# One product of a first-layer pair split into seven smaller ones, with the work around it moved

## The chip, the cores and the metric

The kernel runs on one core of a Trainium2 chip. The core has a matrix engine (TensorE, PE in the profile, with its weight loads shown as PEld), a vector engine (VectorE, DVE), a scalar engine (ScalarE, ACT), a general engine (GpSimd, POOL) and a queue that issues transfers (SyncE, SP). Each takes its instructions in order and waits on semaphores for the others. TensorE writes its results to PSUM, which the kernel uses as eight banks of 512 fp32 words in each of 128 partitions; everything else is in SBUF. The metric is the device time of one execution in microseconds (us), as a median over runs.

## The reference, cut to what matters

```
kv  = einsum('bhsd,bhse->bhde', k, v)    # per batch b (8) and head h (8): k^T v, 64 x 64, over s = 576
out = q kv ; out = out / sqrt(mean(out^2) + 1e-6) * g_norm
x   = out as (B*S, H*D)                  # 4608 tokens x 512 features
y   = (sigmoid(x @ w_gate) * (x @ w_val)) @ w_out     # 512 -> 1536 -> 512, all fp32
```

The two matrix layers of the last line are most of the work. w_gate and w_val are 512 x 1536, w_out is 1536 x 512.

## The kernel before, in words

**Chunks.** The 4608 tokens are cut into nine chunks of 512 (`G`). Chunk 0 is computed plainly while the attention of the first two batches and the conversion of the weights run beside it. Chunks 1 to 8 go through `first_layer_fast(c)` (line 684) and `second_layer_fast(c)` (line 768), in which a product of 2 x 2 blocks is made of seven block products instead of eight, with sums of blocks of x, of the weights and of the results in place of the eighth.

**First layer.** The features are 12 blocks of 128; a pair is block `one` = f and block `two` = f + 6, and there are six pairs in a chunk, so 48 pairs in the eight fast chunks. For each block the 2 x 2 cut of x is by token half (256 tokens, `GH`) and by half of the 512 inputs; that of the weights is by half of the inputs and by gate or value. The seven products are called `p1, p6, p2, p7, p5, p4, p3` and are issued in this order, each for `one` and then for `two`. Each is two matmuls of 128 x 128 weights against 128 x 256 of x (`product`, line 692, the matmul itself on line 694), accumulated in one PSUM bank. An fp32 matmul shows in the profile as two passes, each with a weight load of its own, so a product is four passes and a pair has 56.

`p1` goes to a new bank `pa` and ScalarE copies it (line 702). `p2` adds to `pa`, and ScalarE takes the sigmoid of it for the first token half (line 712). `p6` goes to a new bank `pb`, `p7` and `p4` add to it, and `p5` opens the bank `pc`, to which `p3` adds. After `p6`, `p7`, `p5`, `p4` and `p3` VectorE adds the bank to a sum in SBUF (lines 708, 716, 721, 725, 730), after `p4` ScalarE takes the second sigmoid (line 726). `end` (line 733) multiplies values by gates, 512 wide, once for each block and after all products of the pair, and `h_sums` (lines 763 to 766) forms four sums of results for the second layer, each 256 wide and with both operands in SBUF. Banks are taken in turn from two pools of two (`mm_ps`), four banks in all: the next pair's `p1` goes to the banks of `pb`, its `p6` to those of `pc`. The other four banks are one tile `at` for the attention.

**Weight sums.** `w_sum` (line 677, the instruction on line 681) runs on GpSimd: four subtractions of 128 x 256 for each block, eight in a pair, for the pair that follows. Those of a kind have two buffers, one for each block of a pair, so a sum for the next pair is written when the product that reads the old one is done. They are issued after `p5` (three for each block) and after `p4`.

**Slots.** `feed(b)` makes a list of steps for the attention of batch b = c + 1, and `spread` lays them into a queue `fill`; `slot()` takes one step from it. There are seven slots in a pair (after each of the seven products of both blocks) and 28 in the second layer of a chunk, and a step is issued to its engine at that point of the program. Steps of VectorE go only into slots 2 to 5 of a pair (counted from 0), or 1 to 5 in chunk 1; other slots are left empty or hold a step of another engine. The steps are: turn q (`turn`, line 369, two for each of four head pairs), k^T v (`kv_mm`), its copies out of PSUM (`kv_copies`, line 364, on VectorE), then twice `two_pairs`: `u_mm` on TensorE, `u_square` on ScalarE (line 399), `u_sum` (line 402, two reductions), `u_root` (ScalarE), `u_norm` (line 411, two), and `x_turn` (line 418, two), which also issues the transfers on SP (line 428) that bring the result into the next chunk's x. What does not fit into the 42 slots of the first layer goes on in the second. `sums_of(c + 1)` puts the four x sums of the next chunk (lines 671 to 674) at the end of the queue. Chunks 1 to 6 carry a feed, chunks 7 and 8 none.

Of the kernel before, what the change touches and what calls it, by code (L numbers as in the profile page):

```python
# [20 lines left out]
def kernel(  # L21
# [319 lines left out]
    def feed(b):  # L341
# [4 lines left out]
        def kv_mm():  # L346
            mains, rest = kv_late[b]
            d["kv"] = ps = at_ps()
            for n in range(NHP):
                for j in range(NK4):  # L350
                    for e in range(2):
                        c = slice(NK4 * HD * e + HD * j, NK4 * HD * e + HD * j + HD)
                        nc.tensor.matmul(ps[HD * e:HD * e + HD, n, 0:HD], mains[n, "k"][:, c], mains[n, "v"][:, c],  # L353
                                         start=(j == 0), stop=False)
            for i in range(NHP // 2):
                for r in range(2):
                    for e in range(2):
                        n, rs, c = NHP // 2 * r + i, slice(PH * r, PH * r + PH), HD * (2 * i + e)
                        nc.tensor.matmul(ps[HD * e:HD * e + HD, n, 0:HD], rest[rs, c:c + HD],
                                         rest[rs, GH + c:GH + c + HD], start=False, stop=True)  # L360

        def kv_copies(i, rs):
            for r in rs:
                nc.vector.tensor_copy(out=kvq[QB * r:QB * r + QB, :, i], in_=d["kv"][QB * i:QB * i + QB, :, 0:HD])
# [80 lines left out]
        for i in range(2 * NC):  # L445
            for rs in ((0, 1), (2,)):
                steps.append((DVE, lambda i=i, rs=rs: kv_copies(i, rs)))
# [3 lines left out]
        return steps + [(PE, idle)] + turns_of(n0 + 3) + two_pairs(n0 + 2) + [(PE, idle)] * 5  # L451
# [50 lines left out]
    psum_mm = ctx.enter_context(tc.tile_pool(name="psum_mm", bufs=2, space=bass.MemoryType.PSUM))  # L502
    psum_ctx = tc.tile_pool(name="psum0", bufs=1, space=bass.MemoryType.PSUM)
    psum0 = psum_ctx.__enter__()

    def mm0_ps():
        return psum_mm.tile([P, 512], FP32, tag="mm", name="mm")

    turns = count()

    def mm_ps():
        if next(turns) % 4 < 2:
            return psum.tile([P, 512], FP32, tag="mm", name="mm", bufs=2)
        return mm0_ps()

    def at_ps():
        return psum.tile([P, 4, 512], FP32, tag="at", name="at")
# [145 lines left out]

    def quarters(c):
        return {(i, j): xT[c][:, NK * (j - 1):NK * j, GH * (i - 1):GH * i] for i in (1, 2) for j in (1, 2)}

    def x_sums(c):
# [6 lines left out]
            lambda: tt(out=s[:, 2], in0=a[1, 2], in1=s[:, 1], op=ALU.subtract),  # L674
        ]

# [7 lines left out]
    def first_layer_fast(c):  # L684
        s, a = sx[c], quarters(c)

        def block(f):

            d = {}
            bg, bv = w["wg", f], w["wv", f]  # L690

            def product(ps, wt, xs, new):
                for m in range(NK):
                    nc.tensor.matmul(ps, wt[:, m, :], xs[:, m, :], start=(new and m == 0), stop=(m == NK - 1),  # L694
                                     skip_group_check=True)


            def p1():
                d["pa"] = pa = mm_ps()[:, h1]
                product(pa, bg[:, 0:NK], a[1, 1], True)  # L700
                d["sg"] = sg_tile()
                nc.scalar.copy(out=d["sg"][:, h2], in_=pa)  # L702

            def p6():
                d["pb"] = pb = mm_ps()[:, h1]
                product(pb, tw[f, 2], s[:, 1], True)
                d["h"] = gv_tile(c, f)
                tt(out=d["h"][:, h1], in0=pb, in1=d["sg"][:, h2], op=ALU.add)

            def p2():  # L710
                product(d["pa"], bg[:, NK:], a[1, 2], False)
                nc.scalar.activation(out=d["sg"][:, h1], in_=d["pa"], func=AF.Sigmoid)  # L712

            def p7():
                product(d["pb"], tw[f, 3], a[2, 1], False)
                tt(out=d["h"][:, h2], in0=d["pb"], in1=d["sg"][:, h2], op=ALU.add)  # L716

            def p5():
                d["pc"] = pc = mm_ps()[:, h1]
                product(pc, tw[f, 1], s[:, 0], True)  # L720
                tt(out=d["h"][:, h2], in0=pc, in1=d["h"][:, h2], op=ALU.add)

            def p4():
                product(d["pb"], tw[f, 4], a[2, 2], False)
                tt(out=d["sg"][:, h2], in0=d["pb"], in1=d["sg"][:, h2], op=ALU.add)  # L725
                nc.scalar.activation(out=d["sg"][:, h2], in_=d["sg"][:, h2], func=AF.Sigmoid)  # L726

            def p3():
                product(d["pc"], bv[:, NK:], s[:, 2], False)
                tt(out=d["h"][:, h1], in0=d["pc"], in1=d["h"][:, h1], op=ALU.add)  # L730

            def end():
                tt(out=d["h"], in0=d["h"], in1=d["sg"], op=ALU.mult)  # L733

            return [p1, p6, p2, p7, p5, p4, p3], end

        for f in range(NF2):
            one, two = block(f), block(f + NF2)
            for i, (p, r) in enumerate(zip(one[0], two[0])):
                p()  # L740
                r()
                slot()

                if f + 1 < NF2 or c + 1 < NG:
                    n = (f + 1) % NF2
                    if i == 4:
                        for k_ in (1, 2, 3):
                            w_sum(n, k_)
# [147 lines left out]
```

## Time and profile before

| | |
|---|---|
| median of 9 runs (lowest, highest) | 1081.18 us (1080.71, 1082.5) |
| the profiled execution: its time, its span | 1081.27 us, 1079.4 us |
| TensorE busy, granted clock | 1068.4 us (99%), 0.997 |
| VectorE, GpSimd, ScalarE busy | 636.4, 291.1, 242.4 us |
| first-layer matmuls (line 694) on the chain that ended last | 53% of the span |
| second-layer matmuls (line 780) on it | 25% |

The profile is of one execution. A row of a timeline gives the start, the length from the first start to the last end, and how many instructions are merged in it; the distance from one start to the next is what an instruction costs a full queue, and the duration of a single one is longer, because the end of one overlaps the beginning of the next. A row of groups gives the mean duration of one instruction. The 1.87 us between the span and the time of the profiled execution lie before the first and after the last instruction.

### The profile page before, as it was taken

The page shows a single profiled execution, that of the slowest core. Times are in us where ns is not written, and L with a number is a line of the kernel's source. Part 1 is how long each engine was busy: PE and PEld are TensorE (multiplying, and loading weights), DVE is VectorE, ACT ScalarE, POOL GpSimd, SP SyncE. Part 2 cuts the span into 40 slices and gives each one's busy share as a digit, 9 for nine tenths or more (in the row PEclk, how much of TensorE's full clock was granted, in tenths as well). Part 3 has the DMA queues.
Part 4 walks back from the last instruction along what each step waited for, and adds up shares of the span by engine and source line. Part 5 has one row for each costly group of instructions (what it writes and reads, how often), then busy time and mean ns, then how long its engine had stood idle before and what let it go on. Part 6 is the DMA issues. An engine that isn't in the chain of part 4 may idle for free.

```text
span 1079.4 us, 18246 instructions
## 1 busy us (share of the span) xinstructions
PE 1068.4 (99%) x7226; PEld 886.0 (82%) x7226; DVE 636.4 (59%) x1261; ACT 242.4 (22%) x473; POOL 291.1 (27%) x390
## 2 busy tenths in 40 slices
PE   9999999999999999999999999999999999999997
PEld 8544448888888888888888888888888888888886
DVE  4897757783577437662767357844765266416631
ACT  4654321221113111221122112311131122002200
POOL 0000024440254124420444035402442054205500
PEclk9999999999999999999999999999999999999998
DMA  9944710002400240013201140024001200010001
GB/s 265 246 156 156 243 34 17 12 12 75 119 6 18 58 128 10 24 39 76 81 12 46 42 119 12 20 58 128 1 24 37 48 1 1 2 38 1 1 1 39
DMA packets 69108, 64.89 MB, mean 60 GB/s; under 512 B 23712, under 2 KB 63008, under 8 KB 69024
## 3 DMA queue, kind: packets, MB, share of 16 engines
q1 hardware_dynamic: 68768, 63.69, 20.9%
q8 instruction: 58, 0.95, 0.4%
q14 instruction: 26, 0.21, 0.1%
q10 hardware_dynamic: 256, 0.03, 0.1%
HBM read 47.19 MB, written 9.44 MB: 52 GB/s over the span
## 4 chain that ended last, share of the span: by engine, by line
PE 95%; DVE 2%; DMA 1%; issue 0%; SPq 0%; ACT 0%; DVEq 0%
PE mm L694 53%; PE mm L780 25%; PE mm L541 7%; PE mm L638 4%; PE at L393 2%; PE at L353 1%; PE at L541 1%; DVE gv L733 1%; PE two L291 1%; PE two L261 0%; PE mm L619 0%; PE two L318 0%; DVE qTs L369 0%; DMA q<-in_q_dram 0%; PE two L272 0%
## 5 line engine op out<-in xcount | busy, mean ns | idle before, releaser
L681 POOL TENSOR_TENSOR tw<-gv 128x256 f32<-128x256 f32 x192 | 139.4, 737 | 733.2 <-PE mm L694 581.8
L694 PE MATMUL mm<-xT,tw 128*128 128x256 f32 x768 | 182.1, 380 | 0.0
L694 PE MATMUL mm<-xT,gv 128*128 128x256 f32 x768 | 182.0, 380 | 0.0
L694 PE MATMUL mm<-sx,tw 128*128 128x256 f32 x768 | 181.6, 380 | 0.0
L694 PEld LDWEIGHTS mm<-xT,gv 128*128 128x128 f32 x768 | 145.8, 190 | 20.1 <-issue 0.5
L694 PEld LDWEIGHTS mm<-sx,tw 128*128 128x128 f32 x768 | 146.1, 190 | 19.6
L694 PEld LDWEIGHTS mm<-xT,tw 128*128 128x128 f32 x768 | 145.7, 190 | 19.7
L681 POOL TENSOR_TENSOR tw<-gv,tw 128x256 f32<-128x256 f32 x192 | 157.0, 839 | 0.0
L726 ACT ACTIVATE sg<-sg 128x256 f32<-128x256 f32 x96 | 39.7, 417 | 243.9 <-DVE sg L725 243.7
L733 DVE TENSOR_TENSOR gv<-gv,sg 128x512 f32<-128x512 f32 x96 | 93.7, 1014 | 0.0
L694 PE MATMUL mm<-sx,gv 128*128 128x256 f32 x384 | 90.7, 379 | 0.0
L780 PE MATMUL mm<-w,s 128*128 128x256 f32 (+1 forms) x408 | 88.6, 367 | 0.0
L780 PE MATMUL mm<-t2w,gv 128*128 128x256 f32 x384 | 88.1, 379 | 0.0
L780 PE MATMUL mm<-w,gv 128*128 128x256 f32 x384 | 88.1, 379 | 0.0
L716 DVE TENSOR_TENSOR gv<-mm,sg 128x256 f32<-128x256 f32 x96 | 40.8, 425 | 76.5 <-PE mm L694 76.3
L780 PEld LDWEIGHTS mm<-w,s 128*128 128x128 f32 x408 | 74.1, 191 | 9.3
L694 PEld LDWEIGHTS mm<-sx,gv 128*128 128x128 f32 x384 | 73.1, 190 | 9.8
L780 PEld LDWEIGHTS mm<-w,gv 128*128 128x128 f32 x384 | 73.1, 190 | 9.8
L780 PEld LDWEIGHTS mm<-t2w,gv 128*128 128x128 f32 x384 | 73.0, 190 | 9.7
L541 PE MATMUL mm<-xT,gv 128*128 128x512 f32 x176 | 77.4, 594 | 0.0
L702 ACT COPY sg<-mm 128x256 f32<-128x256 f32 x96 | 35.7, 372 | 156.5 <-PE mm L694 155.3
L712 ACT ACTIVATE sg<-mm 128x256 f32<-128x256 f32 x96 | 36.8, 383 | 125.5 <-PE mm L694 125.5
(96 smaller groups left out, 998.7 us busy)
## 6 DMA issues: line engine op xcount, KB each, us to landing
q<-in_q_dram SPq DMA_DIRECT2D x24, 288.0 KB
st<-in_moe_w_gate_dram SPq DMA_DIRECT2D x12, 512.0 KB
st<-in_moe_w_val_dram SPq DMA_DIRECT2D x12, 512.0 KB
st<-in_moe_w_out_dram SPq DMA_DIRECT2D x12, 512.0 KB
kv<-in_k_dram SPq DMA_DIRECT2D x24, 256.0 KB
kv<-in_v_dram SPq DMA_DIRECT2D x24, 256.0 KB
out_dram<-sg SPq DMA_DIRECT2D x23, 192.0 KB
xT<-xTs SPq DMA_DIRECT2D x48, 72.0 KB
```

The source lines that it names most:

```text
L291: nc.tensor.matmul(d["u"][r:r + PH, e, HD * (i // 2):HD * (i // 2) + HD], d["qT"][es, t0:t0 + PH], kv[es], start=True, stop=True)
L393: nc.tensor.matmul(u[HD * e:HD * e + HD, r, o:o + HD], qTs[QB * r:QB * r + QB, (n0 + which) % 2, c:c + PH], kvq[QB * r:QB * r + QB, (n0 + ...
L541: nc.tensor.matmul(self.ps[i], w[("wg", "wv")[i], self.f][:, m, :], xT[self.c][:, m, :], start=(m == 0), stop=(m == NMT - 1), skip_group_c ...
L638: nc.tensor.matmul(ps[t], gv[0, f][:, P * t:P * t + P], w["wo", f], start=(f == 0), stop=(f == NFT - 1), skip_group_check=True)
L681: nc.gpsimd.tensor_tensor(out=tw[f, i], in0=b[in0], in1=b[in1] if isinstance(in1, tuple) else tw[f, in1], op=ALU.subtract)
L694: nc.tensor.matmul(ps, wt[:, m, :], xs[:, m, :], start=(new and m == 0), stop=(m == NK - 1), skip_group_check=True)
L702: nc.scalar.copy(out=d["sg"][:, h2], in_=pa)
L712: nc.scalar.activation(out=d["sg"][:, h1], in_=d["pa"], func=AF.Sigmoid)
L716: tt(out=d["h"][:, h2], in0=d["pb"], in1=d["sg"][:, h2], op=ALU.add)
L726: nc.scalar.activation(out=d["sg"][:, h2], in_=d["sg"][:, h2], func=AF.Sigmoid)
L733: tt(out=d["h"], in0=d["h"], in1=d["sg"], op=ALU.mult)
L780: nc.tensor.matmul(ps, hs(f), ws[:, f, :], start=(new and f == 0), stop=(f == NF2 - 1), skip_group_check=True)
```

## The change

**The split.** `p2` of `one` and `p2` of `two` multiply the same quarter of x (second half of the inputs, first 256 tokens) with the gate weights of two blocks, so together they are a 256 x 256 by 256 x 256 product. It is now cut once more into 2 x 2 blocks of 128 and made of seven matmuls (`small`, each 128 x 128 weights against 128 x 128 of x) in place of four with 256 columns. Two of the seven add straight into the bank `pa` of `one`; the others go into a fifth bank `pd` (later `pe`). ScalarE copies partial results from it (four copies 128 wide), GpSimd adds two of them (one 256 wide), and VectorE makes three more additions (one 256 wide, two 128 wide). The sigmoid of the first token half now reads SBUF. The weights for it need four more subtractions a pair on GpSimd (`w_sums2`, 128 x 128), the x quarter four more sums a chunk on VectorE (`x_sums2`).

**Banks.** `at` shrinks from four banks to three, and five banks are handed out from a queue, `take` and `give`. `pc` of one block is now the bank of the other's `pa`. `pd` is the third bank in the queue when it is taken: at that point it is the one in which `p3` of `two` of the pair before has just ended.

**Order.** `p5` of `one` comes before `p7`, the weight sums are issued after `p5` of `two`, and `end` is split by token half: that of the second half stands ahead of `p3` of `one` for `one`, and ahead of `p3` of `two` for `two`, there together with the first of the four result sums (`h_sum`); that of the first half stays after all products, with the other three result sums.

**Feed.** The copies of k^T v go from VectorE to ScalarE and are no longer held to slots 2 to 5; the second `two_pairs` gets four empty steps ahead of it, and one of the five empty steps at the end is taken away.

```diff
-                nc.vector.tensor_copy(out=kvq[...], in_=d["kv"][QB * i:QB * i + QB, :, 0:HD])
+                nc.scalar.copy(out=kvq[...].rearrange("p (s n) d -> p s n d", s=2), in_=d["kv"][QB * i:QB * i + QB])
...
-        return steps + [(PE, idle)] + turns_of(n0 + 3) + two_pairs(n0 + 2) + [(PE, idle)] * 5
+        steps += [(PE, idle)] + turns_of(n0 + 3) + [(PE, idle)] * (4 if b > 2 else 0)
+        return steps + two_pairs(n0 + 2) + [(PE, idle)] * 4
...
-        return psum.tile([P, 4, 512], FP32, tag="at", name="at")
+        return psum.tile([P, NQ, 512], FP32, tag="at", name="at")
+    free = deque([4, 2, 3, 0, 1])
+    def take():
+        i = free.popleft()
+        return i, bank(i)[:, 0:GH]
+    def give(i):
+        free.append(i)
...
+        for i, in0, in1 in ((1, b12, b11), (2, b22, 1), (4, b21, 2), (3, b22, b12)):
+            tw2[i] = sums.tile([P, P], FP32, tag=f"tx{i}", name=f"tx{i}", bufs=1)
+            nc.gpsimd.tensor_tensor(out=tw2[i], in0=in0, in1=..., op=ALU.subtract)
...
+            p1(one)
+            p1(two)
+            slot()
+            i_d = free[2]
+            del free[2]
+            pd = bank(i_d)
+            small(pd[:, q1], ones[:, NK], ax[:, 0, q1], True)
+            nc.scalar.copy(out=g1[:, q1], in_=pd[:, q1])
+            small(one["pa"][:, q1], ones[:, NK + 1], ax[:, 1, q1], False)
+            p6(one)
+            small(pd[:, q1], tw2[2], s2[:, 1], False)
+            nc.scalar.copy(out=g2[:, q1], in_=pd[:, q1])
+            small(one["pa"][:, q2], tw2[4], ax[:, 1, q2], False)
+            p6(two)
+            slot()
+            small(pd[:, q1], tw2[3], ax[:, 0, q2], False)
+            nc.scalar.copy(out=g1[:, q2], in_=pd[:, q1])
+            nc.scalar.copy(out=g2[:, q2], in_=pd[:, q1])
+            nc.gpsimd.tensor_tensor(out=g2[:, h1], in0=g2[:, h1], in1=g2[:, h2], op=ALU.add)
+            tt(out=g1[:, h1], in0=one["pa"], in1=g1[:, h1], op=ALU.add)
+            nc.scalar.activation(out=g1[:, h1], in_=g1[:, h1], func=AF.Sigmoid)
+            p5(one, two["ia"])
+            slot()
+            p7(one)
+            pe = bank(i_d)
+            small(pe[:, q1], tw2[1], s2[:, 0], True)
+            tt(out=g2[:, q2], in0=pe[:, q1], in1=g2[:, q2], op=ALU.add)
+            slot()
+            p7(two)
+            p5(two, one["ia"])
+            slot()
...
+            p4(one)
+            small(pe[:, q1], twos[:, NK + 1], s2[:, 2], False)
+            tt(out=g2[:, q1], in0=pe[:, q1], in1=g2[:, q1], op=ALU.add)
+            nc.scalar.activation(out=g2[:, h1], in_=g2[:, h1], func=AF.Sigmoid)
+            p4(two)
+            give(i_d)
+            slot()
...
+            end(one, h2)
+            p3(one)
+            end(two, h2)
+            h_sum(c, f)
+            p3(two)
+            slot()
+            end(one, h1)
+            end(two, h1)
+            h_sums(c, f)
```

## The prediction

> **What bounds the kernel now.** Read first the busy times and the chain that ended last (two lines of the page), then whom TensorE waited for, then its timeline in a stretch of first-layer work and at the very end, where the only passes of 128 columns in the fast part stand.
>
> ```profile
> PE 1068.4 (99%) x7226; PEld 886.0 (82%) x7226; DVE 636.4 (59%) x1261; ACT 242.4 (22%) x473; POOL 291.1 (27%) x390
> ...
> PE 95%; DVE 2%; DMA 1%; issue 0%; SPq 0%; ACT 0%; DVEq 0%
> ```
>
> TensorE is the bound, and 95% of the chain is its own work.
>
> ```profile
> PE mm L619 <- POOL ident masks.py:199: 1.4, 1, 1.4
> PE two L291 <- ACT qTs L277: 0.6, 2, 0.3
> PE two L272 <- DMA q<-in_q_dram: 0.5, 1, 0.5
> ```
>
> These are all the waits of TensorE's matmuls, and none is of the fast layers (lines 694 and 780). So there is no wait to remove: only fewer columns can gain, and every new wait is a loss.
>
> ```profile
> 440.03 2.00 PE L694 MATMUL mm<-xT,tw 128*128 128x256 f32 x8
> 441.86 1.89 PE L694 MATMUL mm<-sx,gv 128*128 128x256 f32 x8
> 443.58 1.89 PE L694 MATMUL mm<-xT,gv 128*128 128x256 f32 x8
> 445.31 1.89 PE L694 MATMUL mm<-sx,tw 128*128 128x256 f32 x8
> ```
>
> ```profile
> 1063.41 2.84 PE L780 MATMUL mm<-w,s 128*128 128x128 f32 x24
> 1066.09 2.76 PE L780 MATMUL mm<-t2w,gv 128*128 128x256 f32 x12
> ```
>
> Sixteen passes of 256 columns go from 441.86 to 445.31: 0.216 us each. Twenty-four of 128 columns, each with its own 128 x 128 weight load, go from 1063.41 to 1066.09: 0.112 us each.
>
> **Step 1, the saving.** In a pair, p2 of both blocks is 4 matmuls = 8 passes x 0.2156 = 1.725 us. The seven small ones are 14 passes x 0.1117 = 1.563 us. Saved: 0.162 us a pair, x 48 pairs = **7.8 us**, all on the path.
>
> [...] This trace has 0.112 against 0.429 for 512 columns (line 541), 58.37 us for 136 passes on its chain, a ratio of 0.26: the weight loads are hidden here. [...]
>
> **Step 2, what VectorE, GpSimd and ScalarE get, and their shared cost.** VectorE, in a pair: one more addition of 256 (0.34 us from start to start in the rows below) and two of 128, which no row shows (bounds 0 and 0.34; nearest, by the slope from 512 wide, 0.60 in 444.13 to 444.73, to 256, 0.34: 0.21 each), and `end` in four parts of 0.34 for two of 0.60: +0.9 us. It loses 12 copies a chunk (72 x 420 ns in the group of line 364), which ScalarE, 22% busy, takes. GpSimd: eight subtractions x 0.69 = 5.5 us before; four of 128 (between 0.35, half of 0.69, and 0.69; I take 0.36, as its two sources scale with width) and one of 256 more: 7.6 us of the pair's 11.9 us (56 x 0.2156 - 0.162). None of this counts by itself: it lies beside TensorE. But look at how the two engines meet:
>
> ```profile
> 221.76 0.74 DVE L402 TENSOR_REDUCE ms<-sqs 128x9 f32<-128x576 f32 x1
> 222.42 0.41 DVE L725 TENSOR_TENSOR sg<-mm,sg 128x256 f32<-128x256 f32 x1
> ...
> 225.22 1.91 DVE L733 TENSOR_TENSOR gv<-gv,sg 128x512 f32<-128x512 f32 x2
> 227.16 0.83 DVE L763 TENSOR_TENSOR s<-gv 128x256 f32<-128x256 f32 x1
> 228.03 0.42 DVE L764 TENSOR_TENSOR s<-s,gv 128x256 f32<-128x256 f32 x1
> 228.37 0.42 DVE L765 TENSOR_TENSOR gv<-gv 128x256 f32<-128x256 f32 x1
> 228.71 0.42 DVE L766 TENSOR_TENSOR s<-gv,s 128x256 f32<-128x256 f32 x1
> ```
>
> ```profile
> 222.15 1.41 POOL L681 TENSOR_TENSOR tw<-gv,tw 128x256 f32<-128x256 f32 x2
> 223.52 1.93 POOL L681 TENSOR_TENSOR tw<-gv 128x256 f32<-128x256 f32 x2
> 225.41 2.31 POOL L681 TENSOR_TENSOR tw<-gv,tw 128x256 f32<-128x256 f32 x2
> ```
>
> ```profile
> 444.13 1.28 DVE L733 TENSOR_TENSOR gv<-gv,sg 128x512 f32<-128x512 f32 x2
> ```
>
> Two `end`s take 1.91 us while GpSimd works and 1.28 us when it rests; the L763 sum takes 0.83 instead of 0.42; GpSimd's two take 2.31 instead of 1.41. L725 beside GpSimd, with one operand in PSUM, stays at 0.41. So VectorE operations with both operands in SBUF and GpSimd's subtractions hold each other up by 0.41 (0.83 - 0.42) to 0.45 us (2.31 - 1.41, halved), a few times a pair.
>
> [...]
>
> Before, the eight subtractions were mostly over when `end` and `h_sums` ran. Now they start after p5 of `two`, last 7.6 us and more, and all eight VectorE operations of that kind (four `end` halves, four sums) fall into the stream. GpSimd: 7.6 + 8 x 0.34 = 10.3 us of 11.9, so it keeps up. Its new addition waits for two ScalarE copies with the next weight sums behind it; these could not start before p5 anyway. Who waits for it is VectorE's 128-wide addition, 1.9 us later in TensorE's time (p5, p7 and a small): hidden.
>
> **Step 3, the new wait.** The first small matmul writes the bank that p3 of `two` has just used, so it waits for VectorE's addition after that p3. Before, such a bank came back with the next p6, three products after its p3 (2.59 us); now it is two (1.73 us), and two `end` halves and a sum stand ahead of that addition. Behind the waiting matmul is all of TensorE's queue, so a wait is paid in full. Count from the end of p4 of `two`: p3, p3, p1, p1 follow, 4 x 0.8625 = 3.45 us. VectorE's p4 addition starts 0.30 us after (p4 of `two` issues until 441.75, L725 starts at 442.06), and the weights must be loaded about 0.16 us ahead (a pass of 0.11 and a semaphore, taken as 0.05): 2.99 us remain. In them stand the p4 addition (0.34), the step of slot 5, and `end`, p3 addition, `end`, sum, p3 addition (4 x 0.34 + 0.42). With a reduction or a normalisation in slot 5 (0.66, from 221.76 to 222.42) that is 2.79 us: it just fits with GpSimd at rest. But `end`, `end` and the sum each may meet GpSimd: 0 to 3 x 0.45 = 1.35 us. So one such place costs between 0 (0.2 us spare; no gain is possible, since TensorE does not wait there now) and 1.15 us. I take the middle of the wait, 0.65, as GpSimd is busy nearly all the time but part of it with short 128-wide operations: **0.45 us a place**.
>
> How many places? The queue laid out by the rule of `spread`, for chunks 2 to 6: slot 5 is empty or ScalarE's or TensorE's in pairs 0, 1 and 2, `u_sum` in pair 3, `u_norm` in pair 4, a `turn` in pair 5, which is followed by the second layer and not by a small matmul. Two places x 5 chunks x 0.45 = **4.5 us**. Without such a step the tail is 2.13 us and 1.35 us of waits are too little to matter much (0.5 over at the very worst). Chunk 1 has a sum of w_out (512 wide, both operands in SBUF) in slot 5 of two pairs, and an `x_turn` ahead of its second layer: bounds 0 and 3 x 1.15; I take **0.5 us** in all.
>
> **Step 4, what costs nothing, and its cover.** ScalarE's copies: the second small into `pd` needs the first copy, with a small and p6 between (1.08 us); a copy is 0.37 us (line 702), and in slot 0 at most one step of that length stands ahead; uncovered it would be some 0.2 us once a chunk. The second u run falls into the second layer before and after; its `x_turn`s and the 24 transfers a chunk that they issue on SP come three slots later, 3 x 6 x 0.216 = 3.9 us; behind them on SP stand the chunk's stores and the next k and v, which are first read 8 slots into the next chunk. The eight x sums now wait for those transfers with one slot less (before: 7.6 us in 5 waits on line 671); VectorE is busy 10.71 of 30 us there, and banks come round in five. If that cover is gone, up to 1.5 us a chunk.
>
> **Sum.** 1081.27 (profiled) - 7.8 + 4.5 + 0.5 = 1078.5; the profiled run lies 0.09 above the median of 1081.18, so 1078.4 us, or 0.26% less.
>
> **The rivals.**
> - *Everything hidden*: the three VectorE operations meet GpSimd at the ends of its operations. For it: 0.2 us spare without meeting. Against: GpSimd will be busy there without a gap. 1081.2 - 7.8 = 1073.4; with up to 3 us of waits, 1076.4.
> - *Slower: VectorE and GpSimd take turns operation by operation.* Then all three wait in full, VectorE goes into the next pair late, and pairs with a step in slots 2 to 4 are late too. At 1.15 us a place and half of it after the other three pairs of a feeding chunk (3 x 6 x 0.55 = 9.9), the waits are 11.5 + 9.9 and the time 1094.8. It turns the sign at 7.8 us of waits, 0.78 us a place in ten places. For it: 225.22 to 228.03, where three in a row paid. Against: the small GpSimd operations, and chunks without a feed.
> - *Evened out*: waits of 5.7 to 10 us, 1079.1 to 1083.3.
> - *The change saves no TensorE time*: small passes come at 0.216 us among 256-wide ones. 14 x 0.2156 - 1.725 = 1.29 us x 48 = +62 us, 1143. Against: at 1063.41 to 1066.09 they do come at 0.112.
>
> **How the numbers follow.** About 0.2% (2.2 us: under 1079.0, over 1083.3) is what a measurement of this kernel can tell from no change. Forecast, waits of 3 to 5.7 us (1076.4 to 1079.1): 0.34; all hidden: 0.21; evened out: 0.25; slower: 0.19; no saving: 0.01. Faster 0.55, same 0.25, slower 0.20. The likeliest is 1078.4. The range 1073.6 to 1084.5 leaves out the top of the slower case and little below; for faster alone it is 1073.4 to 1079.0.
>
> **What would show it.** Small passes 0.112 us apart. TensorE's first waits in the fast layers: line 732 on VectorE, ten of about 0.45 us in pairs 3 and 4 of chunks 2 to 6. No wait in chunks 7 and 8, which then take 2 us less together (12 x 0.162). VectorE's halves of `end` at up to 0.83 us, GpSimd's operations up to 1.18. The prediction is wrong if TensorE waits on GpSimd or ScalarE instead, if waits stand in nearly every pair, or if a wait at line 870 shows.

## The result, and the profile after

The changed kernel takes 1076.21 us (median of 9 runs, 1076.01 to 1077.71) against 1081.32 us for the kernel before (29 runs beside it): a ratio of 0.9952, 95% interval 0.9944 to 0.996. The prediction was 1078.4 us. The profiled execution has a span of 1074.6 us, 4.8 us less than before.

The page's busy line and its chain by engine, after:

```profile
PE 1063.6 (99%) x7514; PEld 884.9 (82%) x7514; DVE 713.0 (66%) x1461; ACT 308.6 (29%) x737; POOL 441.2 (41%) x630
...
PE 97%; DVE 2%; issue 0%; ACT 0%; POOL 0%; DVEq 0%; POOLq 0%
```

TensorE is the bound as before. Line 694 of before is now line 728 (products of 256 columns) and line 732 (the small ones), line 780 is line 870. TensorE's busy time fell by 4.8 us, as the span did; VectorE's rose by 77 us and GpSimd's by 150, beside it. All waits of TensorE's matmuls, after (total us, times, longest us):

```profile
PE mm L634 <- POOL ident masks.py:199: 1.4, 1, 1.4
PE mm L870 <- DVE gv L773: 0.7, 1, 0.7
PE two L291 <- ACT qTs L277: 0.6, 2, 0.3
PE mm L728 <- DVE gv L745: 0.3, 1, 0.3
```

Two are new, in the fast layers (L870, L728), and neither is of line 732. The view counts only time in which no pass is running and drops short waits, so the rest of the reading goes by the distance from one pass to the next. TensorE's timeline after, with small passes among others (start, length, line, instructions merged):

```profile
332.68 1.03 PE L728 MATMUL mm<-sx,tw 128*128 128x256 f32 x4
333.55 0.38 PE L732 MATMUL mm<-xT,tx 128*128 128x128 f32 x2
333.76 1.03 PE L728 MATMUL mm<-sx,tw 128*128 128x256 f32 x4
```

Four passes of 256 columns go from 332.68 to 333.55, 0.217 us each; two of 128 from 333.55 to 333.76, 0.105 each. Over the whole trace the medians are 216 and 111 ns.

Where the time went is seen best by chunk: the distance from the first pass of a chunk's first layer to the first pass of the next one's, in us, worked out from the starts of the passes. (The middle column is experiment 3, which has the feed's two edits and no split.)

| chunk | before | feed edits alone | after |
|---|---|---|---|
| 1 | 115.28 | 115.24 | 116.90 |
| 2 to 6, each | 115.72 to 115.77 | 115.24 to 115.27 | 114.74 to 114.86 |
| 7 | 108.78 | 108.78 | 107.80 |
| 8, first layer | 72.52 | 72.52 | 71.54 |

Chunks 7 and 8 have no feed: they lose 0.98 us each, six pairs at 0.163. That is the saving without any wait, 48 x 0.163 = 7.8 us. Chunks 2 to 6 lose 0.48 more by the feed's edits, and get about 0.5 of new waits, so that they end at -0.96 in the mean. Chunk 1 grows by 1.62: new waits of 2.6 us less the 0.98. The sum, 2 x 0.98 + 5 x 0.96 - 1.62 = 5.1, less 0.4 that is added ahead of chunk 1 (0.20) and behind the last pass of the last second layer (0.18), is the 4.8 of the spans, rounding aside.

The feed's share is the u run (line 393 before, 395 after). Before, its passes take 23.24 us by their distances, after 20.88, and the row that says so stood in the waits of before:

```profile
PEld at L393 <- DVE qTs L369: 1.3, 5, 0.3
```

Five times, in chunks 2 to 6, the weight loads of the second u run waited for VectorE's turn of q. The matmuls' own list, which the prediction read, does not show it; the weight loads' list does. After the change the row is gone.

The new waits of chunks 2 to 6 are short. In TensorE's timeline of chunk 1, two of the longer ones:

```profile
218.56 0.89 PE L728 MATMUL mm<-xT,tw 128*128 128x256 f32 x3 [0.25 <-DVE gv L745]
```

```profile
240.68 0.70 PE L870 MATMUL mm<-w,gv 128*128 128x256 f32 x2 [0.71 <-DVE gv L773]
```

The first is p7, waiting for VectorE's addition after p6; by the distance of starts it is 0.42 us late, and the pass behind it 0.08 more. The second is the second layer, waiting for the last `end` of the chunk's last pair: 0.87 late and 0.10 more on the second pass. In chunks 2 to 6 the waits are 0.01 to 0.09 us, the passes behind them up to 0.1 late in addition, at four places of a chunk, 0.47 us a chunk in all. One of them has another releaser. ScalarE's timeline and then TensorE's, after, in pair 2 of chunk 2:

```profile
305.59 0.36 ACT L365 COPY kvq<-at 32x256 f32<-32x256 f32 x1
305.97 0.27 ACT L791 COPY sg<-mm 128x128 f32<-128x128 f32 x1
```

```profile
306.38 0.46 PE L732 MATMUL mm<-sx,tx 128*128 128x128 f32 x2
```

The copy of the feed (L365) stands ahead of the copy out of `pd` (L791), and the second small product into `pd` comes 0.085 us late, its second pass 0.073: 0.16 us, once a chunk.

What of the place that the prediction feared, pairs 3 and 4 of chunks 2 to 6? VectorE's timeline after, at the end of pair 3 of chunk 2, then GpSimd's:

```profile
328.01 0.74 DVE L404 TENSOR_REDUCE ms<-sqs 128x9 f32<-128x576 f32 x1
328.67 0.42 DVE L773 TENSOR_TENSOR gv<-gv,sg 128x256 f32<-128x256 f32 x1
329.02 0.41 DVE L769 TENSOR_TENSOR gv<-mm,gv 128x256 f32<-128x256 f32 x1
329.35 0.41 DVE L773 TENSOR_TENSOR gv<-gv,sg 128x256 f32<-128x256 f32 x1
329.79 0.56 DVE L847 TENSOR_TENSOR s<-gv 128x256 f32<-128x256 f32 x1
330.28 0.41 DVE L769 TENSOR_TENSOR gv<-mm,gv 128x256 f32<-128x256 f32 x1
330.61 1.48 DVE L773 TENSOR_TENSOR gv<-gv,sg 128x256 f32<-128x256 f32 x2
332.02 0.94 DVE L854 TENSOR_TENSOR s<-s,gv 128x256 f32<-128x256 f32 x1
332.88 0.94 DVE L855 TENSOR_TENSOR gv<-gv 128x256 f32<-128x256 f32 x1
```

```profile
327.82 0.46 POOL L713 TENSOR_TENSOR tx<-gv,gv 128x128 f32<-128x128 f32 x1
328.36 1.05 POOL L713 TENSOR_TENSOR tx<-gv,tx 128x128 f32<-128x128 f32 x2
329.37 0.70 POOL L713 TENSOR_TENSOR tx<-gv 128x128 f32<-128x128 f32 x1
330.04 1.77 POOL L720 TENSOR_TENSOR tw<-gv 128x256 f32<-128x256 f32 x2
```

The step of slot 5 is there as foretold, the reduction at 328.01. But the three operations that could meet GpSimd, `end` (L773) twice and the first result sum (L847), take 0.42, 0.41 and 0.56 us: 0.14 of waiting in all, where the prediction took 0.65. They fall on the four short sums (L713), the second and third of which need the one before: from the end of the first (328.28) to the start of the next (328.36) lie 0.08 us in which GpSimd does nothing. But the first `end` starts inside the second short sum, which ends at 328.81, and still takes 0.42 us, so it is not shown that the gaps are the reason; experiment 5 shows that it matters that the sums there are short ones. The addition that TensorE needs (L769 at 330.28) ends at 330.69, and the small product starts at 330.93, on time: the 0.14 us lie within the 0.2 us that the prediction had to spare. Only behind it, from 330.61 on, against the long sums, do both engines take turns: VectorE's L854 and L855 start 0.86 us apart and last 0.94 each, GpSimd's sums last 0.89 each (1.77 / 2). At that point TensorE has other work.

### The profile page after: what moved, and what is told of

Its sections match the earlier page's. It is cut to its first block, busy times and chain, and to the rows that moved or that the text cites. A ratio compares the mean times of both kernels' runs of the same rounds, so it can differ in the third digit from the quotient of the medians.

```text
span 1074.6 us, 19464 instructions
## 1 busy us (share of the span) xinstructions
PE 1063.6 (99%) x7514; PEld 884.9 (82%) x7514; DVE 713.0 (66%) x1461; ACT 308.6 (29%) x737; POOL 441.2 (41%) x630
## 4 chain that ended last, share of the span: by engine, by line
PE 97%; DVE 2%; issue 0%; ACT 0%; POOL 0%; DVEq 0%; POOLq 0%
PE mm L728 45%; PE mm L870 27%; PE mm L556 7%; PE mm L732 7%; PE mm L653 4%; PE at L395 2%; PE at L354 1%; PE mm L634 1%; PE at L556 1%; PE two L261 1%; PE two L291 1%; PE two L318 0%; PE two L272 0%; DVE gv L773 0%; PE at L360 0%
## 5 line engine op out<-in xcount | busy, mean ns | idle before, releaser
L720 POOL TENSOR_TENSOR tw<-gv 128x256 f32<-128x256 f32 x192 | 156.1, 822 | 233.0 <-DVE w L202 145.3
L728 PE MATMUL mm<-xT,tw 128*128 128x256 f32 x768 | 198.6, 381 | 0.3 <-DVE gv L745 0.3
L728 PE MATMUL mm<-sx,tw 128*128 128x256 f32 x768 | 197.6, 380 | 0.0
L802 POOL TENSOR_TENSOR sg<-sg 128x256 f32<-128x256 f32 x48 | 35.6, 741 | 341.7 <-ACT sg L801 341.6
L728 PEld LDWEIGHTS mm<-xT,tw 128*128 128x128 f32 x768 | 137.4, 191 | 17.8 <-issue 3.4
L728 PEld LDWEIGHTS mm<-sx,tw 128*128 128x128 f32 x768 | 135.1, 191 | 12.2
L773 DVE TENSOR_TENSOR gv<-gv,sg 128x256 f32<-128x256 f32 x192 | 109.7, 590 | 0.0
L728 PE MATMUL mm<-sx,gv 128*128 128x256 f32 x384 | 91.3, 381 | 0.0
L728 PE MATMUL mm<-xT,gv 128*128 128x256 f32 x384 | 90.8, 380 | 0.0
L870 PE MATMUL mm<-w,gv 128*128 128x256 f32 x384 | 89.2, 381 | 0.7 <-DVE gv L773 0.7
L870 PE MATMUL mm<-t2w,gv 128*128 128x256 f32 x384 | 88.7, 381 | 0.0
L870 PE MATMUL mm<-w,s 128*128 128x256 f32 (+1 forms) x408 | 88.3, 367 | 0.0
L870 PEld LDWEIGHTS mm<-w,gv 128*128 128x128 f32 x384 | 72.6, 190 | 12.0 <-DVE gv L773 2.6
L870 PEld LDWEIGHTS mm<-w,s 128*128 128x128 f32 x408 | 74.2, 191 | 9.3
L728 PEld LDWEIGHTS mm<-xT,gv 128*128 128x128 f32 x384 | 73.0, 190 | 10.2 <-issue 0.5
L728 PEld LDWEIGHTS mm<-sx,gv 128*128 128x128 f32 x384 | 72.7, 190 | 9.9
L870 PEld LDWEIGHTS mm<-t2w,gv 128*128 128x128 f32 x384 | 72.5, 190 | 9.8
L745 DVE TENSOR_TENSOR gv<-mm,sg 128x256 f32<-128x256 f32 x96 | 37.0, 413 | 40.7 <-PE mm L728 40.7
```

The source lines that it names most:

```text
L720: nc.gpsimd.tensor_tensor(out=tw[f, i], in0=b[in0], in1=b[in1] if isinstance(in1, tuple) else tw[f, in1], op=ALU.subtract)
L745: tt(out=d["h"][:, h1], in0=d["pb"], in1=d["sg"][:, h2], op=ALU.add)
L773: tt(out=d["h"][:, h], in0=d["h"][:, h], in1=d["sg"][:, h], op=ALU.mult)
L802: nc.gpsimd.tensor_tensor(out=g2[:, h1], in0=g2[:, h1], in1=g2[:, h2], op=ALU.add)
L870: nc.tensor.matmul(ps, hs(f), ws[:, f, :], start=(new and f == 0), stop=(f == NF2 - 1), skip_group_check=True)
```

## The experiments

Theory: the split saves 7.8 us, the feed's edits 2.4, and what is given back (about 5 us) comes from VectorE being late against TensorE, because its operations with both operands in SBUF meet GpSimd's sums and take longer. Rivals: the given-back part comes from the order of the work (banks, chains), or the feed is the whole gain.

**1. The second u run at its old place, rest as changed.**

```diff
-        steps += [(PE, idle)] + turns_of(n0 + 3) + [(PE, idle)] * (4 if b > 2 else 0)
-        return steps + two_pairs(n0 + 2) + [(PE, idle)] * 4
+        return steps + [(PE, idle)] + turns_of(n0 + 3) + two_pairs(n0 + 2) + [(PE, idle)] * 5
```

> The changed kernel with one part undone: the second u run stands where it did before (no four empty steps ahead of it, five at the end). In the profile of before the second u run's weight loads stood idle for a turn of q (line 369, five times), and its passes took 23.2 us in all against 20.9 us after the change. Theory 'the move of the second u run gained about 2.4 us, which I had costed at nothing': 1076.2 + 2.4 = 1078.6 us, with gaps of about 0.35 us back in the u run of chunks 2 to 6. Rival 'those gaps were closed by the lighter VectorE queue (k^T v copies gone to ScalarE), not by the move': within 0.5 us of 1076.2.

Measured: 1089.65 us, ratio to before 1.0075 (1.0061 to 1.0089). The mechanism is there, more than five times its size. TensorE's waits, then its windows just after the u runs of chunks 2 and 5 (start:end, length, busy time and passes, granted clock, DMA share, GB/s):

```profile
PE at L395 <- DVE qTs L371: 8.5, 5, 1.7
```

```profile
359.40:363.40 4.00, 4.00 (x12) 0.57 0.20 66
...
711.40:715.40 4.00, 4.00 (x12) 0.57 0.21 68
```

The u run waits 1.9 us (by distances) in each of five chunks, 9.5 us, for the turn of q (L371); in the kernel before the same wait was 0.35 us at most, by the same distances. And after two of the five idles the granted clock is 0.50 for 3.4 us, from 359.86 to 363.27 and from 711.43 to 714.84 (the 0.57 is the mean of a 4 us window that takes in a little more): 256-column passes come 427 ns apart instead of 216, 3.4 us lost in all. 9.5 + 3.4 is 12.9 of the 13.4 us between the two kernels. The move of the u run, priced at nothing, is worth 13 us in the changed kernel.

The five gaps are 1.7 us long each (no pass running; 8.5 us in all in the first row above): two of them were followed by the lower clock, three were not.

**2. The move of the u run alone, in the kernel before.**

```diff
-        return steps + [(PE, idle)] + turns_of(n0 + 3) + two_pairs(n0 + 2) + [(PE, idle)] * 5
+        steps += [(PE, idle)] + turns_of(n0 + 3) + [(PE, idle)] * (4 if b > 2 else 0)
+        return steps + two_pairs(n0 + 2) + [(PE, idle)] * 4
```

> The kernel before with one part of the change alone: four empty steps ahead of the second u run, one fewer at the end. Theory 'the move alone gains': 1081.3 - 2.4 = 1078.9 us, line 393's passes 20.9 us in place of 23.2. Rival 'the gaps close only with the rest of the change': 1081.3 within 0.5 us, since the turn that the u run waits for comes from a VectorE queue that is as full as before.

Measured: 1082.31 us, ratio 1.0006 (0.9997 to 1.0014). Theory and rival both missed by number: it is 1.06 us slower than the kernel before beside it (1081.25), which the interval does not tell from no change. The u runs take 20.83 us, so its 2.4 us are gained; the second layer gives 3.6 back. TensorE's waits and VectorE's timeline:

```profile
PE mm L781 <- DVE sg L797: 2.8, 2, 1.4
```

```profile
615.09 0.69 DVE L672 TENSOR_TENSOR sx<-xT 128x512 f32<-128x512 f32 x1 [6.86 <-DMA xT<-xTs]
...
616.42 0.42 DVE L797 TENSOR_TENSOR sg<-mm,sg 128x256 f32<-128x256 f32 x1
```

The x sum of the next chunk (L672) stands on VectorE waiting 6.86 us for the transfer of x that now comes later, behind it the addition L797, and behind that the second layer, 1.6 us late in two chunks. This is the cover that step 4 named: x sums behind later transfers.

**3. Both edits of the feed in the kernel before, no split.** The edit of experiment 2, and

```diff
-                nc.vector.tensor_copy(out=kvq[...], in_=d["kv"][...])
+                nc.scalar.copy(out=kvq[...], in_=d["kv"][...])
...
-                steps.append((DVE, lambda i=i, rs=rs: kv_copies(i, rs)))
+                steps.append((ACT, lambda i=i, rs=rs: kv_copies(i, rs)))
```

> The kernel before with both edits of the feed (copies of k^T v on ScalarE, second u run four slots later) and without the split. My theory: the two edits belong together, because 12 copies a chunk less in VectorE's slots bring the rest of the feed forward; the waits in the u run (2.4 us) vanish and at least part of the 3.6 us of second-layer waits that the move alone brought vanishes with them: between 1078.9 us (1081.3 - 2.4, all second-layer waits gone) and 1081.5 us. The split's own share of the gain is then 2.7 us (1078.9 - 1076.2) or more. Rival: the feed's edits are the whole gain and the split gives back all it saves: within 0.7 us of 1076.2.

Measured: 1078.78 us, ratio 0.9975 (0.9965 to 0.9985). The changed kernel on the same chip took 1076.54 (experiment 12). So the feed gives 2.6 us, and the split on top of it 2.2: it saves 7.8 and gives 5.6 back. The rival that the feed is the whole gain falls; the two intervals touch (0.9965 to 0.997), but the table shows the split's 0.98 in chunks 7 and 8, which have no feed. The split without the feed's edits was not run. No matmul of the fast layers waits in this kernel, and the table by chunk has it: 0.48 us in each of chunks 2 to 6, next to nothing in the others. Adding the copies' move, 12 copies a chunk off VectorE, closes the second-layer wait of experiment 2.

**4. The copies of k^T v back on VectorE, rest as changed.**

```diff
-                nc.scalar.copy(out=kvq[...].rearrange("p (s n) d -> p s n d", s=2), in_=d["kv"][...])
+                nc.vector.tensor_copy(out=kvq[...].rearrange("p (s n) d -> p s n d", s=2), in_=d["kv"][...])
...
-                steps.append((ACT, lambda i=i, rs=rs: kv_copies(i, rs)))
+                steps.append((DVE, lambda i=i, rs=rs: kv_copies(i, rs)))
```

> The changed kernel with the copies of k^T v back on VectorE, in its slots 2 to 5, and all else as changed. Twelve copies a chunk are 12 x 0.34 = 4 us of VectorE's queue, and since they may stand only in slots 2 to 5 the steps after them come later. Theory 'VectorE has little room in the feeding chunks, so this part is needed': waits of 0.2 to 0.6 us in line 728 or 732 where the copies stand, and reductions in other slots: 1077 to 1080 us. Rival 'the copies are hidden on either engine': within 0.7 us of 1076.2.

Measured: 1087.2 us, ratio 1.0063 (1.0049 to 1.0078): beyond both expectations. TensorE's waits, and VectorE's timeline at the end of pair 1 of chunk 2:

```profile
PE mm L732 <- DVE gv L769: 6.5, 13, 1.2
PE mm L870 <- DVE sg L886: 3.2, 2, 1.7
```

```profile
304.20 0.42 DVE L365 COPY kvq<-at 32x256 f32<-32x256 f32 x1
304.65 0.51 DVE L773 TENSOR_TENSOR gv<-gv,sg 128x256 f32<-128x256 f32 x1
305.19 0.42 DVE L769 TENSOR_TENSOR gv<-mm,gv 128x256 f32<-128x256 f32 x1
305.54 0.64 DVE L773 TENSOR_TENSOR gv<-gv,sg 128x256 f32<-128x256 f32 x1
306.21 0.83 DVE L847 TENSOR_TENSOR s<-gv 128x256 f32<-128x256 f32 x1
306.96 0.41 DVE L769 TENSOR_TENSOR gv<-mm,gv 128x256 f32<-128x256 f32 x1
```

This is the wait that step 3 describes: a step in slot 5 (here the copy L365), then `end`, addition, `end`, sum, addition, with 0.10 + 0.23 + 0.41 = 0.74 us of waiting on GpSimd where 0.65 was taken, and the small product (L732) starts 0.43 us late, its second pass 0.10 more. It stands at ten places of chunks 2 to 6 (after pairs 1 and 2; one of them 1.24 us), and with 0.9 to 1.4 us at three of chunk 1; the rest is second layer (3.2). So the predicted mechanism exists, near the predicted price, but at pairs whose slot 5 the copies' move has emptied.

**5. The short sums behind the long ones.** In the changed kernel `w_sums2` goes behind the last of the three kinds of long sums after p5:

```diff
-                w_sums2(n)
                 for i in (n, n + NF2):
                     w_sum(i, 3)
+                w_sums2(n)
             p4(one)
```

> The changed kernel with GpSimd's order turned: the two 256-wide sums for p7 stand ahead of the four 128-wide ones, so that long operations run on GpSimd while VectorE's tail (the two halves of end and the first result sum) passes. Theory 'the waits that I had forecast after pairs 3 and 4 did not come because the tail met the four short sums, each of which waits for the one before it, and not the long ones': the tail now meets operations of 0.73 us, and the first small matmul (line 732) waits 0.2 to 0.9 us after pairs 3 and 4 of chunks 2 to 6, 2 to 9 us in all: 1078 to 1085 us. Rival 'VectorE has time enough there whatever GpSimd runs': within 0.7 us of 1076.2.

Measured: 1077.31 us, ratio 0.996 (0.9946 to 0.9974). TensorE's waits, then VectorE's timeline at the same end of pair 3 as above:

```profile
PE mm L732 <- DVE gv L769: 1.1, 2, 0.5
```

```profile
327.99 0.84 DVE L773 TENSOR_TENSOR gv<-gv,sg 128x256 f32<-128x256 f32 x1
...
330.01 0.41 DVE L769 TENSOR_TENSOR gv<-mm,gv 128x256 f32<-128x256 f32 x1
```

The two waits of the view stand in chunk 1. The first `end` now takes 0.84 us instead of 0.42, and by distances the ten places appear, at 0.24 + 0.10 us each: 3.4 us. The whole, 1077.31, lies between the two expectations (1078 or more; at most 1076.9): it loses only 1.1, below the changed kernel's spread, because other waits fell: by distances line 728's from 2.3 to 0.7 us and line 870's from 2.4 to 1.2. The place is shown, the time not beyond doubt.

**6. All of `h` at once, after the last products**, as before the change, with the split and the feed as changed:

```diff
-            end(one, h2)
             p3(one)
-            end(two, h2)
-            h_sum(c, f)
             p3(two)
             slot()
-            end(one, h1)
-            end(two, h1)
+            end(one, slice(0, G))
+            end(two, slice(0, G))
+            h_sum(c, f)
             h_sums(c, f)
```

> The changed kernel with one part undone: h is finished at once, 512 wide and after the last products, and all four result sums after it. Theory 'the halves ahead of the last products are needed, because after them VectorE and GpSimd take turns and the next pair's additions come late': the tail before the first small matmul gets shorter by three operations (about 1 us), but two 512-wide and four 256-wide operations with both operands in SBUF then meet GpSimd's stream, 6 x 0.45 us more on VectorE ahead of the additions after p6; TensorE waits in line 728 in most pairs of feeding chunks, 0.2 to 0.5 us each, 30 pairs: 1082 to 1091 us. Rival 'the split of end only moves work and is worth nothing on TensorE': within 1 us of 1076.2; or, if the tail was what cost, about 1 us less.

Measured: 1085.99 us, ratio 1.004 (1.0027 to 1.0053). Half of `h` ahead of the last products is worth 9.8 us. TensorE's waits:

```profile
PE mm L728 <- DVE gv L745: 5.6, 23, 0.4
```

By distances 67 passes of line 728 are late, 13.5 us in all: after most pairs the six operations (two `end`s of 512 and four sums) come in one block while GpSimd is busy, and the addition after p6 of the next pair (L745) is late. Chunks 7 and 8, which have no feed, pay 2.3 us each, so it needs no feed steps. The page's row of `end`:

```profile
L773 DVE TENSOR_TENSOR gv<-gv,sg 128x512 f32<-128x512 f32 x96 | 106.2, 1145 | 0.0
```

**7. GpSimd's weight sums only for the first pair.** The kernel keeps using the sums of the first pair.

```diff
-            if more:
+            if False:
                 for k_ in (1, 2):
...
-            if more:
-                for i in (n, n + NF2):
-                    w_sum(i, 4)
```

> The changed kernel without the weight sums of all pairs but the first (every later pair reads the first pair's, so the numbers are not the reference's; GpSimd keeps only its addition of line 802). TensorE, VectorE and ScalarE do the same work in the same order. In the profile of the changed kernel TensorE loses about 5.0 us to waits in the fast layers that before did not have (2.6 us in chunk 1, 0.47 us in each of chunks 2 to 6). Theory 'they come from VectorE and GpSimd holding each other up': nearly all go, 1076.2 - 4 = 1072 us (1071.2 to 1073), and VectorE's halves of end last 0.42 us instead of 0.59. Rival 'VectorE is late by its own work': the waits stay, 1075 to 1076.5 us.

Measured: 1071.89 us, ratio 0.9918 (0.9903 to 0.9933). The page's busy line of it:

```profile
PE 1059.6 (99%) x7514; PEld 886.6 (83%) x7514; DVE 623.9 (58%) x1461; ACT 308.6 (29%) x737; POOL 45.5 (4%) x66
```

VectorE does the same 1461 instructions in 89 us less, and TensorE is busy 4.0 us less: nearly all of the waits described above are gone. 1071.89 is near the sum without waits, 1081.3 - 7.8 - 2.4 = 1071.1; so 4.3 of some 5 us go. The rows of the halves of `end`, in the changed kernel and here:

```profile
L773 DVE TENSOR_TENSOR gv<-gv,sg 128x256 f32<-128x256 f32 x192 | 109.7, 590 | 0.0
```

```profile
L773 DVE TENSOR_TENSOR gv<-gv,sg 128x256 f32<-128x256 f32 x192 | 75.6, 414 | 0.0
```

The mean falls from 590 to 414 ns, while the additions with one operand in PSUM (L763) stay at 423. VectorE does not wait for results of GpSimd: the list of its waits has no such row in the changed kernel, nor in the kernel before. So it is the operations that get longer.

**8. Both: all of `h` at once and no weight sums** (the edits of 6 and 7).

> The run with h finished at once after the last products (1086.0 us), and without the weight sums of all pairs but the first, as in the run above (later pairs read the first pair's sums). That run waits 13.5 us in line 728. Theory 'those waits are the meeting of VectorE's two-operand work with GpSimd's stream': without the stream they go, 1071 to 1074 us, the same as the run above within 1 us. Rival 'it is the order alone, VectorE finishing late what the next pair needs': the waits stay, 1083 to 1086 us.

Measured: 1072.68 us, ratio 0.9918 (0.9906 to 0.993). An `end` of 512 takes 683 ns in the mean, where it took 1145 in experiment 6. What cost 9.8 us beside GpSimd's sums costs 0.8 without them. This separates the theory from the rival: the order of `end` and the sums matters only while the two engines meet.

**9. Slot 5 free of VectorE's feed steps.**

```diff
-            spread(steps, (1, 2, 3, 4, 5) if c == 1 else (2, 3, 4, 5))
+            spread(steps, (1, 2, 3, 4) if c == 1 else (2, 3, 4))
```

> The changed kernel with one rule of the feed changed: VectorE's steps may stand in slots 1 to 4 in chunk 1 and 2 to 4 in the others, no longer in slot 5, the one just ahead of the tail. Of the 5.0 us of waits left, 2.6 us stand in chunk 1, where sums of the weights of the second layer and an x turn stand in slot 5; in chunks 2 to 6 the waits are 0.47 us each. Theory 'what stands in slot 5 makes the tail late': chunk 1 gains 1 to 2 us and the others up to 0.2 us each: 1073.5 to 1075.5 us. Rival 'the work only moves, and the steps that run over into the second layer make its end late': 1076 to 1079 us.

Measured: 1074.62 us, ratio 0.9938 (0.9924 to 0.9953), the profiled execution with a span of 1071.0, 3.6 less than the changed kernel's. Chunk 1 takes 115.64 us in place of 116.90, and chunks 2 to 6 some 0.33 less each. Only one wait of size is left in the fast layers, and its row names it, the sums of the second layer's weights in chunk 1:

```profile
PE mm L870 <- DVE t2w L939: 1.0, 1, 1.0
```

**10. The same, with those sums sooner in chunk 1.**

```diff
-                    i += 3
+                    i += 2
-            spread(steps, (1, 2, 3, 4, 5) if c == 1 else (2, 3, 4, 5))
+            spread(steps, (1, 2, 3, 4) if c == 1 else (2, 3, 4))
```

> The changed kernel with VectorE's feed steps kept out of slot 5, and in chunk 1 the sums of the second layer's weights laid in after every second step of the feed and not after every third. With slot 5 free but the sums as they were, one wait of 1.16 us was left in chunk 1, of the second layer for the last of these sums. My theory: it goes, and the time is 1071.5 to 1073.8 us against 1074.6. Rival: the turns of q in chunk 1 come later for it and the u run waits instead: 1074.6 or more.

Measured: 1077.96 us, ratio 0.9961 (0.9949 to 0.9973): worse than 9, and the theory fell. The wait on L939 is gone and 0.38 us of waiting remain there, but the first u run of chunk 1 comes 24 us later than in experiment 9, and with it the transfers of x and the x sums of chunk 2. TensorE's waits, then its windows at the start of chunk 2:

```profile
PE mm L728 <- DVE sx L692: 1.3, 1, 1.3
...
PE mm L732 <- DVE sx L702: 0.6, 1, 0.6
```

```profile
278.00:280.60 2.60, 1.97 (x8) 0.80 0.84 233
280.60:282.60 2.00, 2.00 (x8) 0.50 1.01 335
```

The first layer of chunk 2 waits for the x sums, 1.46 and 0.79 us by distances, and the granted clock is 0.50 for 3.4 us from 279.58 on; the second window lies inside that. It is the rival's kind of price, paid at the x sums and not in the u run: chunk 2 takes 4.0 us more than in experiment 9. Chunk 4 takes 1.0 more, where the second layer's addition (L894) stands behind an x sum that waits for its transfer.

**11 and 12. Experiment 9 once more, and the changed kernel beside it.** The edit of 9; and none.

> The changed kernel with VectorE's feed steps kept out of slot 5, run once more beside the changed kernel itself, since their intervals overlapped. My theory: the wait for the first small products' predecessors and the turns between VectorE and GpSimd at the end of a pair cost 1 to 2.5 us: 1073.7 to 1075.2 us. Rival: the first figure was spread, within 0.5 us of the changed kernel.

> The changed kernel itself, on the same chip as the three others: 1075.7 to 1077.7 us by either theory. It is the measure for the kernel with slot 5 free.

Measured: 1074.85 us, ratio to before 0.9935 (0.9923 to 0.9947), and 1076.54 us, ratio 0.9957 (0.9944 to 0.997). The difference of 1.7 us came twice (1.6 the first time), though the intervals still touch; slot 5 free is the fastest version that does all of the work. Its profiled execution here had a span of 1074.0, 3.0 more than the first one. TensorE's waits and VectorE's timeline show where half of that is:

```profile
PE mm L870 <- DVE sg L894: 1.4, 1, 1.4
```

```profile
616.00 0.69 DVE L691 TENSOR_TENSOR sx<-xT 128x512 f32<-128x512 f32 x1 [4.29 <-DMA xT<-xTs]
...
617.34 0.41 DVE L894 TENSOR_TENSOR sg<-mm,sg 128x256 f32<-128x256 f32 x1
```

In one chunk the transfer of x landed late (VectorE waits 4.29 us for it, 2.09 in the first profile), and the second layer's addition stood behind the x sum: the chain of experiment 2, now once, for 1.64 us with its second pass. Another 0.7 us of the 3.0 lie ahead of chunk 1 and 0.5 in one u run. So a run of this version can pay for a late transfer; the changed kernel's profiled execution of the result did not.

## Why the prediction was right or wrong

**Step 1, the saving: right.** 7.8 us taken; 0.163 us a pair in chunks 7 and 8 measured, 7.8 us. The small passes come 111 ns apart among the others (0.1117 taken).

**Step 2, the two engines: right in kind.** VectorE's operations with both operands in SBUF meet GpSimd, and experiments 7 and 8 show that 4.3 of the some 5 us that are given back hang on it. Two sizes were off. Where they take turns with the long sums, an operation costs 0.86 us from start to start, 0.52 more than the 0.34 at rest, and not 0.41 to 0.45 more. And beside the short sums little is lost (0.14 us at the place shown).

A pair of operations, one on each engine, takes 0.86 us in turns, where the two rows at rest add up to 0.34 + 0.69 = 1.03 us. And the 0.36 us of a short sum rested on its cost going with its width, which no run shows: from start to start it takes 0.41 us at least in the changed kernel, and 0.53 where the next sum needs it.

**Step 3, the new wait: the term that failed.** Ten places at 0.45 us, 4.5 in all, were taken; they waited nothing. The error is the 0.65 us of meeting GpSimd "as GpSimd is busy nearly all the time": 0.14 was measured, since there the short sums run, and that lies within the 0.2 us to spare. Two smaller slips of the same sum cancel: p4 of `two` issues until 441.86, where the next product starts, and not 441.75, which gives 0.10 us more room; and the first result sum needs the second `end` and starts 0.44 us after it, and not 0.34. The 0.05 us of a semaphore, taken without a row, holds: after the change, at the end of pair 3 of chunk 2, the addition that the first small product waits for ends at 330.689 and the product's weight load starts at 330.743. Experiments 4 and 5 show the same place paying 0.34 to 0.53 us when the occupation of slot 5 or the order on GpSimd is another. The total of new waits came out right by accident: 5.0 us were taken, 2.6 in chunk 1 plus 5 x 0.5 is 5.1 measured. Chunk 1 got 0.5 in the forecast and cost 2.6: the kind that was priced, the first small product waiting for the addition after p3, came at 0.55, and 2.1 stood in the middle of pairs (lines 728, 732) and at the second layer, which were not priced at all. VectorE has feed steps in up to five slots of a pair there; freeing slot 5 (experiment 9) takes away 1.3 of the 2.6. The prediction's own sign of failure, "if a wait at line 870 shows", did show, and so, at 0.16 us a chunk, did a wait on ScalarE.

**Step 4, what costs nothing: wrong on the feed, in the direction of a gain.** The gain of 2.4 us in the second u run was missing, though the row of weight loads waiting for the turn of q was there to be read. Since the total of the waits came out right by accident, this is the whole miss: 1078.4 - 2.4 is 1076.0, against 1076.2. ScalarE's copy uncovered at 0.2 us once a chunk was named and measured at 0.16. The x sums behind later transfers, "up to 1.5 us a chunk", stayed covered in the changed kernel's profile and cost 1.6 us in each of two chunks of experiment 2. That the feed's edits hold the rest up, 13 us for the u run's place and 11 for the copies, inside the changed kernel, was not seen by any step.

**The rivals.** "Everything hidden" (1073.4 to 1076.4) holds the measured time, but not for its reason: 5 us of waits are there, and 2.4 us from elsewhere pay for half of them. The forecast's own class, waits of 3 to 5.7 us, holds the waits, while the time lies 0.2 us under its 1076.4. "Slower by turns" did not come; experiment 6 is what it looks like, at 1086. "No saving" fell with the 111 ns.

## What to carry to other kernels

Read the waits of the weight loads beside those of the matmuls: TensorE's waits stand in two lists, and the row that explained half of the gain (L393, 1.3 us of waits, gone after a change by which its passes take 2.4 us less) stood only in the second. What VectorE lost to GpSimd went in these runs by what stood in GpSimd's stream at that moment, 0.14 us on three operations beside the short sums and 0.52 us on each in turns with the long ones, in one execution with GpSimd 41% busy; so look at which of its operations run there, long or short. And edits of a schedule are not worth a fixed amount: the u run's move gave nothing alone, 2.6 us together with the copies' move, and 13 us beside the split, so price an edit in the kernel it will stand in.

## What the runs showed of the hardware

- After an idle of 1.7 us TensorE got a clock of 0.50 for 3.4 us in two cases of five (experiment 1), and the same around waits of 1.46 and 0.79 us that lie within 2.6 us (experiment 10, from 279.58 on).
- The waits of matmuls in the changed kernel cost more than themselves: the second pass of the same matmul comes 0.07 to 0.10 us late in addition (0.08 at 218.86 behind a wait of 0.42, 0.10 at 241.00 behind one of 0.87). The same 0.10 stands behind attention matmuls without any wait, three times in each of chunks 1 to 6, before the change too.
- VectorE (both operands in SBUF) and GpSimd in turns, in the changed kernel from 332.02 on: one operation of 256 of each every 0.86 us, where they need 0.34 (VectorE) and 0.69 (GpSimd) from start to start alone.
- GpSimd's 128 x 128 subtraction took 0.46 us alone (at 327.82 in the changed kernel), against 0.73 for 128 x 256, and each of the 96 that need the result of the one before started 0.08 us after its end.
